# Reordering the two ends of a fused gradient kernel: power tables and dense layer moved into the FFT phase, row products moved into the first inverse

## The chip, the cores and the metric

The kernel runs on one core of a Trainium2 chip. The metric is the device time of one execution in microseconds (us). The kernel is one program of some 20,000 instructions on five engines: TensorE (PE; its weight loads are shown apart as PEld), VectorE (DVE), ScalarE (ACT), GpSimd (POOL) and SyncE (SP). Each engine has its own stream of instructions. The kernel's author writes one sequence of operations; a scheduler then decides, from that sequence and a plan of times of its own, in which order the instructions stand on each engine. So a change in the sequence can move instructions on engines that it does not mention.

## The reference

The forward function mixes two branches by a gate, and the reference returns its output together with the gradients for 14 inputs. L = 2048 positions, D = 448 channels, N = 256 states, F = 1792 hidden features.

```python
def _A_ref(u, A_re, A_im, B_re, B_im, C_re, C_im, log_dt, Dskip):
    dt = jnp.exp(log_dt)[:, None]
    ...
    P = jnp.exp(logdA[:, :, None] * l[None, None, :])      # powers of lambda
    K = jnp.einsum("dn,dnl,dn->dl", Cc, P, dB).real        # one kernel of L taps per channel
    ...                                                    # zero-padded FFTs of K and u
    y = irfft2(Uf * Kf)[..., :L]
    return y.transpose(0, 2, 1) + u * Dskip

def _B_ref(x, w1, b1, w2, b2):
    h = jnp.einsum("bsd,df->bsf", x, w1) + b1
    r = jnp.where(h > 0, h, 0)
    return jnp.einsum("bsf,fd->bsd", r * r, w2) + b2

g = _sigmoid((x * gate_w).sum(-1, keepdims=True))
out = g * _A_ref(x, ...) + (1 - g) * _B_ref(x, ...)

def reference(...):
    _out, _vjp = jax.vjp(_f, A_u, A_A_re, ..., gate_w)
    return (_out, *_vjp(grad_out))
```

## The kernel before

The kernel runs in phases:

1. *Front*: load u, the gate, DA = g x grad_output; an FFT in two layers of u and of DA, each layer going through DRAM (`fwd1` writes `gd`, `fwd2` reads it back); their product, and the inverse in two layers (`inv1` writes `hd`, `inv2`), give dk, the gradient of the kernel's taps. Beside it the raw parameters are turned into lambda and its powers (`powers`), which go to DRAM as records `rec_d`.
2. *Channel loop*: 14 blocks of 32 channels. For each, tables X and Y of powers are built by doubling (VectorE), the taps K are made from them (`kgen`, TensorE), and the gradients for the states are contracted with dk (`back_z`, `back_p`). Between these the dense branch runs forward and backward (`hidden`, `project`, and the weight gradients `grad_w2`, `grad_w1`).
3. *Tail*: FFT of K, two inverses (the output y, and the gradient of u), the parameter gradients, and some sums over rows.

The order of the front, cut to what the change touches (F17, K28, X16 and so on are buffers in on-chip memory that several tiles share in turn; a new tile of a name waits until the old one is no longer read):

```python
    for g in range(NG):                                   # u: four loads of 32 rows
        (nc.sync if g % 2 == 0 else nc.scalar).dma_start(flat(U[32 * g:32 * g + 32]), tl(u2, g))
    ...
    for t in range(LT):                                   # L362: the gate's row sums
        V.scalar_tensor_tensor(out=junk[:, 0, :], in0=U[:, t, 0:D], scalar=1.0, in1=gw_bc[:], ..., accum_out=s32[:, t:t + 1])
    S.activation(g_b[:], s_b[:], ACT.Sigmoid)             # L365
    for t in range(LT):
        last_da = V.tensor_scalar(out=DA[:, t, :], in0=G[:, t, :], scalar1=g32[:, t:t + 1], ...)
    ...
    K.act_only = True                                     # ScalarE alone empties the banks
    K.fwd1(lambda j: U[:, j, 0:D], gd[0], stage[0])
    K.act_only = False                                    # ScalarE and VectorE in turn (L171, L172, L181, L183)
    K.fwd1(lambda j: DA[:, j, :], gd[1], stage[1])
    transposed(U, None)
    ...
    for nm, src in (("Ar", A_A_re), ...):                 # raw parameters into X16
        nc.sync.dma_start_transpose(out=r, in_=src)
    ...                                                   # some 15 us of VectorE work on X16, Y16: L453 to L475
    for t in range(LT):
        S.activation(DB[:, t, :], G[:, t, :], ACT.Copy, scale=omg32[:, t:t + 1])
    transposed(DB, DBT_d)
    S1t = [K.t("X16", [P, 8192]), K.t("Y16", [P, 8192])]  # the buffers of fwd2's loads
```

The dense layer's first half, the powers and the loop over the four quarters of the spectrum:

```python
    def hidden(j):
        for l2 in range(2):
            for lc in (2 * l2, 2 * l2 + 1):
                ps = K.ps(NT[nti % 3], [P, 512])          # three accumulation banks in turn: N0, N1, N2
                ... T_.matmul(ps[:], lhsT=w1w[...], rhs=UT[...]) ...       # L501, L504
            for k in range(2):
                S.activation(RX[rxi % 3][...], pss[k][:], ACT.Relu, bias=b1_f[:, j:j + 1])   # L507
            G_.dma_start(... rT_d ..., RX[rxi % 3])
    psets = [(Fp[:, 0:4 * RS], ...), (RA[:, 0:4 * RS], ...)]   # powers' buffers: F17, and part of R32

    def powers(gr):
        rb, cb, qb = psets[gr % 2]
        ...
        for k in range(NLEV):                             # 11 levels, ScalarE and VectorE in turn
            S.copy(dst..., x)                             # L551
            if k < NLEV - 1:
                S.activation(sq, x, ACT.Square)           # L554
                V.scalar_tensor_tensor(...)               # L555
                V.tensor_tensor(...)                      # L556
        nc.scalar.dma_start(... rec_d ..., R)

    def spectra(q):
        for w in range(2):
            s1 = s1r[n1 % 4]
            K.load_s1(gd[w], q, s1)                       # L205
            K.fwd2(s1, q, spw[:, 2 * (q % 2) + w])        # L215
            ...
    spectra(0)
    for q in range(4):
        if q < 3:
            spectra(q + 1)
        K.cmul(Pc, ...)                                   # L227 to L232
        K.inv1(Pc, q, hd[0])                              # L246
        powers(q)
    dk_tl = K.t("D16", [P, LT, D])
    DK = K.t("K28", [P, 32, D])
    for q in range(4):
        hs = s1r[n1 % 4]...
        K.load_hs(hd[0], q, hs)
        ... K.inv2(...); K.evac2(dk_tl[...], ps)          # L264
    for rep in range(2):                                  # L599: dk spread over the partitions
        for g in range(NG):
            (nc.sync if rep == 0 else G_).dma_start(DK..., dk_tl...)
    for j in range(4):
        hidden(j)
```

The channel loop, in outline (L626, L627, L632 are the three products of a doubling; L684 is `kgen`; L713 and L726 empty the turned tables; L743 scales dk; L754 and L757 are `back_z`, L776 and L785 `back_p`):

```python
    for c in range(NCH + 1):
        ... seeds_x(c); ax = build_x(c); tables_t(c, 0)
        ... back_p(c - 1, ..., back_z(c - 1, YTs[c - 1], (0, 1)), ...)
        for half in range(2):
            ay = build_y(c, half, ap or ax)
            if half == 1:
                k_out(c, kgen(c))
            YTs[c] += [(turn_yt if g == 3 or c in (0, NCH - 1) else load_yt)(g) for g in (2 * half, 2 * half + 1)]
        ...
    for j in range(4, FT):
        hidden(j)
```

The tail's rows and inverses:

```python
    for g in range(NG):
        nc.sync.dma_start(flat(Gt[32 * g:32 * g + 32]), tl(G2, g))
    GU = K.t("Y16", [P, LT, D])
    V.tensor_tensor(out=GU[:], in0=Gt[:], in1=Uv, op=ALU.mult)          # L1148
    for t in range(LT):
        T_.matmul(ps[0:1, 0:D], lhsT=omg_b[:, t:t + 1], rhs=Gt[:, t, :], ...)   # L1152
    for t in range(LT):
        T_.matmul(ps[0:1, 0:D], lhsT=g_b[:, t:t + 1], rhs=GU[:, t, :], ...)     # L1157
    GK = K.t("Y16", [P, LT, D])
    V.tensor_tensor(out=GK[:], in0=Gt[:], in1=dskb, op=ALU.mult)        # L1161
    ...
    for q in range(4):                                                  # first inverse: the output
        for x in range(2):
            for hp in range(2):
                K.inv2(hs, q, x, hp, ps, [(ident[:], A[:, t, :]), (negI[:], br)])   # L262, L264
                V.scalar_tensor_tensor(out=jk, in0=ps, in1=Gt[:, t, :], ..., accum_out=dg[:, t:t + 1])  # L1185
                V.scalar_tensor_tensor(out=A[:, t, :], in0=ps, scalar=g32[:, t:t + 1], in1=br, ...)
        if q < 2:
            product(1, q + 2, sx[q + 2])
        ...
    for q in range(4):                                                  # second inverse, with GK: gradient of u
        ...
```

Of the kernel before, what the change touches and what calls it, by code (L numbers as in the profile page):

```python
# [129 lines left out]
class Ker:  # L130
# [56 lines left out]
    def fwd1(self, rhs, gd, stage):  # L187
        nc = self.nc
        for hh in range(2):
            for q in range(4):  # L190
                st = stage[self.stage_i % len(stage)]
                self.stage_i += 1
                for j2 in range(2):
                    ps = self.pair()
                    for jj in range(2):
                        nc.tensor.matmul(ps[jj][:, 0:D], lhsT=self.F1[:, hh * 128:(hh + 1) * 128], rhs=rhs(q * 4 + j2 * 2 + jj), start=True, stop=True)
                    self.evac2(st[:, 2 * j2:2 * j2 + 2, :], ps)
                j0base = 32 * hh + q * 4
                for g2 in range(2):
                    dst = bass.AP(tensor=gd, offset=(j0base + 16 * g2) * 64 * D, ap=[[D, 64], [64 * D, 4], [1, D]])  # L200
                    (self.q2 if g2 == 0 else nc.sync).dma_start(dst, st[g2 * 64:(g2 + 1) * 64])

    def load_s1(self, gd, q, s1):
        src = bass.AP(tensor=gd, offset=8 * q * D, ap=[[32 * D, 128], [1, 8 * D]])
        self.nc.sync.dma_start(s1.rearrange("p a d -> p (a d)"), src)  # L205
# [64 lines left out]
def kernel(ctx, tc, A_u, A_A_re, A_A_im, A_B_re, A_B_im, A_C_re, A_C_im, A_log_dt, A_Dskip,  # L270
# [54 lines left out]
    for g in range(NG):  # L325
        (nc.sync if g % 2 == 0 else nc.scalar).dma_start(flat(U[32 * g:32 * g + 32]), tl(u2, g))
# [9 lines left out]
    load_const("M2", nc.scalar)  # L336
# [61 lines left out]
    K.act_only = True  # L398
    K.fwd1(lambda j: U[:, j, 0:D], gd[0], stage[0])
    K.act_only = False  # L400
    K.fwd1(lambda j: DA[:, j, :], gd[1], stage[1])
    transposed(U, None)
# [7 lines left out]
    o = 0  # L410
# [3 lines left out]
    prm = [K.t("X16", [P, 8192]), K.t("Y16", [P, 8192])]  # L414
    raw = {}
    o = 0

    def carve(n, dt=bf16, k=0):
        nonlocal o
        w = n * (2 if dt == fp32 else 1)  # L420
        if k:
            r = prm[k][:, 0:w]
        else:
            r = prm[0][:, o:o + w]
            o += w
        return r.bitcast(fp32) if dt == fp32 else r
    for nm, src in (("Ar", A_A_re), ("Ai", A_A_im), ("Br", A_B_re), ("Bi", A_B_im), ("Cr", A_C_re), ("Ci", A_C_im)):
        r = carve(2 * D).rearrange("p (h d) -> p h d", h=2)
        nc.sync.dma_start_transpose(out=r, in_=src)
        raw[nm] = r  # L430
# [45 lines left out]

    for t in range(LT):
        S.activation(DB[:, t, :], G[:, t, :], ACT.Copy, scale=omg32[:, t:t + 1])
# [13 lines left out]
    def hidden(j):  # L492
        nonlocal nti, rxi
        for l2 in range(2):
            pss = []
            for lc in (2 * l2, 2 * l2 + 1):
                ps = K.ps(NT[nti % 3], [P, 512])
# [68 lines left out]
    def spectra(q):  # L566
        nonlocal n1
        for w in range(2):
            s1 = s1r[n1 % 4]
            n1 += 1  # L570
            K.load_s1(gd[w], q, s1)
            sp = spw[:, 2 * (q % 2) + w]
            K.fwd2(s1, q, sp)
            dst = bass.AP(tensor=sp_d[w], offset=q * 4 * 2 * D, ap=[[16 * 2 * D, P], [1, 8 * D]])
            nc.scalar.dma_start(dst, sp.rearrange("p a r d -> p (a r d)"))
    spectra(0)
    for q in range(4):
# [5 lines left out]
        powers(q)  # L583
    dk_tl = K.t("D16", [P, LT, D])
    DK = K.t("K28", [P, 32, D])
    for q in range(4):
        hs = s1r[n1 % 4].rearrange("p (g x) d -> p g x d", g=4)
        n1 += 1
# [13 lines left out]
    for j in range(4):  # L602
        hidden(j)
# [113 lines left out]
    def turn_yt(g):  # L717
# [4 lines left out]
        for h in range(2):  # L722
            pt = K.ps("X", [P, CW, P], bf16)
# [80 lines left out]
    for c in range(NCH + 1):  # L804
# [13 lines left out]
        for half in range(2):  # L818
            if c < NCH:
# [4 lines left out]
                YTs[c] += [(turn_yt if g == 3 or c in (0, NCH - 1) else load_yt)(g) for g in (2 * half, 2 * half + 1)]  # L824
# [5 lines left out]
    for j in range(4, FT):  # L830
        hidden(j)
# [109 lines left out]
    for g in range(NG):  # L941
        G_.dma_start(U[32 * g:32 * g + 32, :, 0:D], tl(u2, g).rearrange("p (t d) -> p t d", d=D))
# [54 lines left out]
    for j in range(FT):  # L997
        grad_w2(j)
    for j in range(JS):
# [147 lines left out]
    GU = K.t("Y16", [P, LT, D])  # L1147
    V.tensor_tensor(out=GU[:], in0=Gt[:], in1=Uv, op=ALU.mult)  # L1148
    row = K.t("st", [1, 3, D], bufs=2)
    ps = K.ps("N0", [P, 512])  # L1150
    for t in range(LT):
        T_.matmul(ps[0:1, 0:D], lhsT=omg_b[:, t:t + 1], rhs=Gt[:, t, :], start=(t == 0), stop=(t == LT - 1))  # L1152
    S.copy(row[:, 0], ps[0:1, 0:D])
    nc.sync.dma_start(out_13.rearrange("(o d) -> o d", o=1), row[:, 0])
    ps = K.ps("N1", [P, 512])
    for t in range(LT):
        T_.matmul(ps[0:1, 0:D], lhsT=g_b[:, t:t + 1], rhs=GU[:, t, :], start=(t == 0), stop=(t == LT - 1))  # L1157
    S.copy(row[:, 1], ps[0:1, 0:D])
    nc.sync.dma_start(out_9.rearrange("(o d) -> o d", o=1), row[:, 1])
    GK = K.t("Y16", [P, LT, D])  # L1160
    V.tensor_tensor(out=GK[:], in0=Gt[:], in1=dskb, op=ALU.mult)  # L1161
# [9 lines left out]
    brq = [load_br(0, 0), load_br(0, 1)]  # L1171
    for q in range(4):
# [16 lines left out]
        if q < 2:  # L1189
            product(1, q + 2, sx[q + 2])  # L1190
        sl = lambda a: a[:].rearrange("p (h q x) -> p q h x", h=2, q=4)[:, q]
# [69 lines left out]
```

## Time and profile before

| quantity | value |
|---|---|
| three timed executions | 1044.84, 1050.16 and 1068.91 us, median 1050.16 |
| the profiled execution | 1046.11 us, its span 1044.3 us |
| mean granted TensorE clock | 0.825 of full speed |
| bytes moved by DMA | 189.24 MB, mean 181 GB/s |
| fewest bytes a packet | 89473 of 151682 packets are under 512 B |

A line of the profile that speaks of an operation names its line in the kernel (L626), the engine, the operation and the tiles as "written <- read". Tiles are named by the first letters of their buffer (F for F17, K for K28, psN for a bank N0 to N3, psX for the bank X). Waits are put down to the operation whose end released the waiting one. A slice of the page's overview is a fortieth of the span, 26.1 us, and its digit gives the busy share in tenths.

### The profile page before, as it was taken

To read this page: it belongs to the slowest core of one execution; us is meant where nothing else is said; L and a number is where in the kernel's file an instruction comes from. 1 tells how busy PE (TensorE), PEld (TensorE's weight loads), DVE (VectorE), ACT (ScalarE), POOL (GpSimd) and SP (SyncE) were. 2 spreads that over 40 slices of the span, in tenths; PEclk is the share of its full clock that TensorE was granted. 3 is DMA by queue.
4 is the path that set the end of the run, shared out by engine and by line. 5 is a ranking of instruction groups with operands and counts; after the bars stand their busy time and mean duration, and the time that the engine had idled before them with its cause. 6 is when DMAs were issued, how large, how long until landed. Compare 5 with 4: busy or idle time off the path is not lost.

```text
span 1044.3 us, 20210 instructions
## 1 busy us (share of the span) xinstructions
PE 765.4 (73%) x8201; PEld 367.3 (35%) x8201; DVE 828.0 (79%) x1150; ACT 692.2 (66%) x1053; POOL 212.3 (20%) x358
## 2 busy tenths in 40 slices
PE   3655642649896898889889886078888976777886
PEld 1222210124343454444344334044545533323322
DVE  3588986584999989979799889189999678997470
ACT  0795558648878897677466646188687756765445
POOL 1330000101121221513423332002112421211120
PEclk9766555569898999789899987569899997889978
DMA  8979557972469557355956869742653679669788
GB/s 210 236 214 382 202 190 214 229 216 87 120 162 155 154 144 159 117 132 170 171 131 171 129 172 134 124 93 78 144 128 117 191 259 351 191 223 280 198 252 219
DMA packets 151682, 189.24 MB, mean 181 GB/s; under 512 B 89473, under 2 KB 124341, under 8 KB 150565
## 3 DMA queue, kind: packets, MB, share of 16 engines
q1 hardware_dynamic: 107956, 78.36, 33.9%
q0 software_dynamic: 24656, 78.65, 26.0%
q10 hardware_dynamic: 18976, 30.94, 8.5%
q8 instruction: 64, 1.05, 0.5%
q14 instruction: 30, 0.24, 0.1%
HBM read 94.45 MB, written 69.54 MB: 157 GB/s over the span
## 4 chain that ended last, share of the span: by engine, by line
DVE 33%; DMA 20%; PE 20%; ACT 14%; issue 10%; POOL 2%; SPq 0%; ACTq 0%; DVEq 0%; POOLq 0%
DVE F L627 5%; DMA R<-Y 4%; DVE P L776 3%; DVE Y L626 2%; DVE X L626 2%; ACT R L757 2%; PE psN L846 2%; DMA K<-D 2%; DVE Y L632 2%; DVE X L632 2%; DMA s_d<-st 2%; PE psX L684 2%; DMA gd<-F 2%; DMA R<-br_d 2%; DVE R L1071 1%
## 5 line engine op out<-in xcount | busy, mean ns | idle before, releaser
L757 ACT CAST R<-psF 128x1024 bf16<-128x1024 f32 x112 | 115.0, 1027 | 34.3 <-PE psF L754 32.4
L776 DVE TENSOR_TENSOR P<-R 128x2048 bf16<-128x2048 bf16 x84 | 98.0, 1219 | 37.1 <-ACT R L757 37.1
L846 PE MATMUL psN<-D,S 128*128 128x448 bf16 x448 | 107.0, 376 | 13.2 <-ACT D L847 10.1
L713 ACT COPY R<-psX 128x1024 bf16<-128x1024 bf16 x56 | 57.1, 1019 | 40.7 <-PE psX L712 40.4
L626 DVE TENSOR_TENSOR Y<-Y,F 128x256 bf16<-128x256 bf16 (+2 forms) x84 | 72.7, 866 | 2.3
L632 DVE TENSOR_TENSOR Y<-Y,F 128x256 bf16<-128x256 bf16 (+2 forms) x84 | 72.6, 864 | 2.2
L626 DVE TENSOR_TENSOR X<-X,F 128x512 bf16<-128x512 bf16 (+3 forms) x56 | 64.9, 1160 | 9.6 <-ACT F L653 7.8
L627 DVE TENSOR_TENSOR F<-Y,F 128x256 bf16<-128x256 bf16 (+2 forms) x84 | 72.0, 857 | 0.5
L969 PE MATMUL psN<-D,S 128*128 128x448 bf16 x224 | 55.9, 380 | 15.0 <-ACT S L964 11.2
L632 DVE TENSOR_TENSOR X<-X,F 128x512 bf16<-128x512 bf16 (+3 forms) x56 | 64.9, 1159 | 1.7
L627 DVE TENSOR_TENSOR F<-X,F 128x512 bf16<-128x512 bf16 (+3 forms) x56 | 64.5, 1151 | 0.1
L969 PEld LDWEIGHTS <-S 128*128 128x128 bf16 x448 | 41.4, 104 | 63.9 <-issue 20.9
L501 PE MATMUL psN<-S,U 128*128 128x512 bf16 x168 | 52.8, 428 | 14.7 <-ACT S L507 5.7
L846 PEld LDWEIGHTS <-S 128*128 128x128 bf16 x448 | 40.5, 102 | 62.7 <-issue 30.5
L754 PE MATMUL psF<-R,K 64*32 64x256 bf16 x672 | 38.0, 353 | 33.1 <-DMA R<-Y 26.9
L921 PE MATMUL psN<-S,U 128*128 128x512 bf16 x168 | 50.0, 421 | 6.2 <-ACT S L926 6.2
L969 PE MATMUL psX<-U,S 128*128 128x449 bf16 x192 | 48.5, 395 | 4.3 <-ACT S L964 4.3
L754 PEld LDWEIGHTS <-K 64*32 64x32 bf16 x896 | 25.8, 152 | 73.6 <-issue 42.3
L712 PE MATMUL psX<-ident,X 128*128 128x128 bf16 x448 | 39.8, 235 | 14.2 <-DVE X L632 8.0
L785 PE MATMUL psS<-P,cb_sel 128*32 128x256 bf16 x336 | 44.5, 285 | 1.5 <-DVE P L776 1.2
L785 PE MATMUL psN<-P,cb_sel 128*32 128x256 bf16 x336 | 45.3, 286 | 0.0
L726 ACT COPY M<-psX 128x1024 bf16<-128x1024 bf16 x28 | 28.7, 1026 | 19.1 <-PE psX L725 19.1
(332 smaller groups left out, 1898.1 us busy)
## 6 DMA issues: line engine op xcount, KB each, us to landing
hd<-st ACTq DMA_DIRECT2D x20, 448.0 KB, 5.4
sp<-K ACTq DMA_DIRECT2D x8, 896.0 KB, 8.3
S<-rT_d POOLq DMA_DIRECT2D x8, 896.0 KB, 6.9
dhT_d<-S POOLq DMA_DIRECT2D x28, 256.0 KB, 4.0
S<-rT_d POOLq DMA_DIRECT2D x14, 512.0 KB, 4.4
S<-dhT_d POOLq DMA_DIRECT2D x14, 512.0 KB, 6.1
R<-sp SPq DMA_DIRECT2D x8, 896.0 KB, 5.5
R<-hd SPq DMA_DIRECT2D x16, 448.0 KB, 6.8
```

Source lines behind the costliest of these rows:

```text
L501: T_.matmul(ps[:], lhsT=w1w[:, dt, j * P:j * P + P], rhs=UT[:, dt, 512 * lc:512 * lc + 512], start=(dt == 0), stop=False, skip_group_check ...
L626: V.tensor_tensor(out=hi, in0=lo, in1=bcast_dims(pr, [0, (None, n // 2), 1]), op=ALU.mult)
L627: V.tensor_tensor(out=Vv.rearrange("p (x a q) -> p x a q", x=rows, q=2), in0=lo, in1=bcast_dims(pi, [0, (None, n // 2), 1]), op=ALU.mult)
L632: return V.tensor_tensor(out=T4[:, :, :, n:2 * n], in0=T4[:, :, :, n:2 * n], in1=V4, op=ALU.add)
L713: S.copy(XT[:, gg].rearrange("p t i n -> p (t i n)"), pt[:].rearrange("p a n -> p (a n)"))
L754: T_.matmul(psz[32 * ii:32 * ii + 32, t, 256 * s:256 * s + 256], lhsT=(DK[64 * t:64 * t + 64, :, d] if s == 0 else DKB[64 * t:64 * t + 64, ...
L757: S.copy(zb[:, :, :, i2, :], psz[:].rearrange("p t (s n) -> p t s n", s=2))
L776: lastp = V.tensor_tensor(out=pr.rearrange("p t s i n -> p t s (i n)"), in0=zv, in1=(xb if r == 0 else rev_dim(xb, 1)), op=ALU.mult)
L785: T_.matmul(sps[s][32 * gr:32 * gr + 32, r, :], lhsT=sel[:, k, off:off + 32], rhs=Q[r][:, t, s, i2, :], start=(g < 2 and cc == 0 and i2 == ...
L846: T_.matmul(ps[:, 0:D], lhsT=hblk[j][:, P * tt:P * tt + P], rhs=ws[:, j, :], start=(w == 1 and j == 0), stop=(j == FT - 1))
L921: T_.matmul(ps[:], lhsT=w2Tw[:, jp, dt, j % 2], rhs=dblk[:, dt], start=(dt == 0), stop=False, skip_group_check=True)
L969: T_.matmul(ps[:, 0:width], lhsT=hh[:, t, :], rhs=(DB2[:, t, :] if w == 0 else U[:, t, 0:D + 1]), start=(t == 0), stop=(t == LT - 1))
```

## The change

It has four aims: to begin the gate sooner (u comes in two halves, and five of the eight stages of its first FFT layer are emptied by ScalarE alone, the others by both engines), to give VectorE its parameter work before the second `fwd1`, to bring the powers and the first four parts of the dense layer into the FFT phase, on the two banks X and S that this phase leaves free, and to take work on grad_output off the start of the tail's first inverse.

```diff
-    for g in range(NG):
-        (nc.sync if g % 2 == 0 else nc.scalar).dma_start(flat(U[32 * g:32 * g + 32]), tl(u2, g))
+    for h in range(2):
+        for g in range(NG):
+            src = bass.AP(tensor=u2.tensor, offset=u2.offset + (16 * g + 8 * h) * D, ap=[[64 * D, 32], [1, 8 * D]])
+            (nc.sync if g % 2 == 0 else nc.scalar).dma_start(flat(U[32 * g:32 * g + 32, 8 * h:8 * h + 8]), src)
 ...
-    load_const("M2", nc.scalar)
+    for nm, src in (("Ar", A_A_re), ("Ai", A_A_im), ...):      # moved here from below
+        nc.sync.dma_start_transpose(out=r, in_=src)
+    load_const("M2", nc.sync)
 ...
-    K.act_only = True
-    K.fwd1(lambda j: U[:, j, 0:D], gd[0], stage[0])
-    K.act_only = False
-    K.fwd1(lambda j: DA[:, j, :], gd[1], stage[1])
-    transposed(U, None)
+    K.fwd1(lambda j: U[:, j, 0:D], gd[0], stage[0], 5)         # act_only for the first 5 stages
 ...                                                            # the parameter work
+    K.fwd1(lambda j: DA[:, j, :], gd[1], stage[1])
+    transposed(U, None)
     for t in range(LT):
         S.activation(DB[:, t, :], G[:, t, :], ACT.Copy, scale=omg32[:, t:t + 1])
 ...
-    def hidden(j):
+    def hidden(j, banks):
-                ps = K.ps(NT[nti % 3], [P, 512])
+                ps = K.ps(banks[nti % len(banks)], [P, 512])
 ...
-            K.load_s1(gd[w], q, s1)
+            K.load_s1(gd[w], q, s1, G_ if w == 0 and q < 2 else None)
 ...
+    powers(0)
     spectra(0)
+    powers(1)
     for q in range(4):
         ...
         K.inv1(Pc, q, hd[0])
-        powers(q)
+        if q < 2:
+            powers(q + 2)
+    for j in range(4):
+        hidden(j, NT[4:6])                                     # banks X and S
     ...
-        hs = s1r[n1 % 4].rearrange("p (g x) d -> p g x d", g=4)
-        n1 += 1
+        hs = spw[:, q].rearrange("p a r d -> p (a r) d").rearrange("p (g x) d -> p g x d", g=4)
 ...
-    for j in range(4):
-        hidden(j)
 ...
-                YTs[c] += [(turn_yt if g == 3 or c in (0, NCH - 1) else load_yt)(g) for g in (2 * half, 2 * half + 1)]
+                for g in (2 * half, 2 * half + 1):
+                    YTs[c].append(turn_yt(g, ("S", "N3")) if c == 0 else turn_yt(g) if g == 3 or c == NCH - 1 else load_yt(g))
 ...                                                            # gradient phase: the second load of u
-    for g in range(NG):
-        G_.dma_start(U[32 * g:32 * g + 32, :, 0:D], tl(u2, g).rearrange("p (t d) -> p t d", d=D))
     for j in range(FT):
         grad_w2(j)
+        if j == 8:
+            for g in range(NG):
+                G_.dma_start(U[32 * g:32 * g + 32, :, 0:D], tl(u2, g).rearrange("p (t d) -> p t d", d=D))
 ...                                                            # tail
-    GU = ...; the 16 + 16 row matmuls and their outputs; GK = ...     # before the first inverse
     for q in range(4):
         ...
         if q < 2:
             product(1, q + 2, sx[q + 2])
+        if q == 1:
+            GU = ...; the 16 + 16 row matmuls and their outputs
+        if q == 3:
+            GK = ...
```

## The prediction

> **What bounds the kernel now.** I read first the page's busy shares and its 40 slices, to find which engine is nearly full and where it is not.
>
> ```profile
> PE 765.4 (73%) x8201; PEld 367.3 (35%) x8201; DVE 828.0 (79%) x1150; ACT 692.2 (66%) x1053; POOL 212.3 (20%) x358
> DVE  3588986584999989979799889189999678997470
> PEclk9766555569898999789899987569899997889978
> ```
>
> No engine is full, VectorE (DVE) is nearest. One digit stands for 26.1 us. From slice 10 to slice 32 VectorE stands at 7 to 9 except for one slice (number 25, 653 to 679 us). The change touches little there. What it does touch are slices 0 to 9 (0 to 261 us) and the last three. So I took the busy time of these stretches (columns: PE, PEld, DVE, ACT, POOL with counts, clock, DMA share, GB/s):
>
> ```profile
> 0.00:16.00 16.00, 0.18 (x1) 0.13 (x2) 0.32 (x3) 1.28 (x1) 3.06 (x11) 1.00 0.85 178
> 16.00:40.00 24.00, 15.29 (x77) 6.73 (x76) 16.80 (x57) 9.48 (x20) 4.72 (x5) 0.79 0.99 223
> 40.00:60.00 20.00, 13.93 (x69) 6.09 (x67) 14.03 (x25) 18.50 (x32) 8.42 (x14) 0.78 0.98 282
> 105.00:165.00 60.00, 34.76 (x120) 9.59 (x118) 54.37 (x108) 37.10 (x65) 0.00 (x0) 0.50 0.51 193
> 165.00:202.00 37.00, 12.54 (x77) 2.94 (x78) 17.32 (x47) 25.48 (x54) 1.75 (x4) 0.50 0.88 240
> 228.00:246.00 18.00, 16.63 (x118) 6.52 (x119) 3.18 (x3) 17.05 (x26) 3.50 (x7) 0.89 0.51 180
> ```
>
> VectorE works 169.6 us in the first 246 us: the six rows above hold 106.0 us of it, the three rows between them (60 to 82, 82 to 105 and 202 to 228) 17.9, 20.5 and 25.2. It idles 76 us, which is the whole room of the front part. Then the waits of that stretch say what ended the idle time (engine, line, what it waited for, total, times, longest):
>
> ```profile
> DVE X L640 <- PE psX L684: 16.9, 1, 16.9
> DVE st L362 <- DMA U<-in_A_u_dram: 14.9, 1, 14.9
> DVE R L172 <- PE psN L196: 9.8, 2, 9.4
> ACT g_b L365 <- DVE s_b L364: 17.3, 1, 17.3
> ACT F L653 <- DMA rec_d<-F: 7.2, 1, 7.2
> SPq L205 <- DVE X L469: 14.9, 1, 14.9
> ```
>
> Last the chain of waits, in order of time, which shows why the first channel block's kernel rows (L684) come at 245.9:
>
> ```profile
> 184.79 12.39 DMA rec_d<-F
> 204.78 21.62 DMA K<-D
> 229.10 6.83 DMA rT_d<-S
> 245.89 2.23 PE psX L684 x127
> ```
>
> The reader is to see a chain, not a full engine: a store of power records holds the buffer F until 197.2; the evacuations of dk stand behind that wait in ScalarE's order; then the spread of dk (K from D) takes 21.6 us; then ScalarE's scaling of it (L743), the dense layer's relus and the turned tables come before L684. VectorE has finished table Y at 231.3 and starts the next table X at 248.1.
>
> [...] ScalarE idles 17.3 us behind the sigmoid (L365) although the banks it is to empty next were filled by 18.2 us. So the order of instructions on an engine is itself the thing that this change edits. [...] here the granted clock is 0.50 from 105 to 202 us, and the second FFT layer's matmul of 448 columns takes 580 ns there, while a dense-layer matmul of 512 columns takes 379 ns at its median. [...] with a DMA share of 0.98 from 16 to 60 us I give the two loads moved to GpSimd nothing. [...] the trace has 1219 ns (L776), and 3.89 us for the two products of the tail, so moving those saves a place in line, not work.
>
> **The change, part by part.** I looked also at the order of the changed program's instructions on each engine. Nothing is added in arithmetic; everything is a matter of place.
>
> (1) u in two halves. The load takes 13.9 us to 15.6. If half the bytes land in half that time, the 16 row sums of the gate (0.67 us each) start near 9 us. Eight are done when the second half lands; the other eight with four transposition copies between them (0.69 each) end at about 15.6 + 8 x 0.67 + 4 x 0.69 = 23.7, against 29.2. Worth 5 us, if the load of grad_output, issued right behind, does not mix in.
>
> (2) Parameters before the second first-layer FFT. VectorE idled 9.4 us until the first of these banks (34.1 to 43.5). Now about 15 us of parameter work stands there, and the raw parameters are fetched before the constant M2. It also releases the buffers X and Y: the loads of the second layer waited 14.9 us for L469. But the DMA share is 0.98 in this time, and the 3.7 MB of that layer's own store move later. I take 8 us.
>
> (3) Powers ahead. From 105 to 202 VectorE works 54.4 + 17.3 = 71.7 of 97 us. Groups 2 and 3 of the powers ended that stretch alone, in turns with ScalarE at 0.76 us of waiting per level, and the store of group 2 held buffer F, which cost the start of table X 7.8 us. In the changed order groups 0 and 1 stand before and among the first evacuations, 2 and 3 among the complex products; the tables follow at once. Of the 25 us idle I expect 15 back; the rest is the inverse's own chain.
>
> (4) Dense layer on X and S, dk and kernel rows. L684 now stands on TensorE before the first use of dk, and L743 on ScalarE behind the rows' output. So the 16.9 us wait should all but go, but dk is still needed for the first P product (L776, at 262.3, which is 60.7 us after table X began at 201.7). Count in the new order from the start of table X: two X tables at 14 us, Y at 14.4, L684 at 2.2 make 45. For dk: of the eight pairs of dense-layer banks (four calls, two each) seven stand on TensorE just ahead of dk's matmuls or among them. Such a pair, with only two banks, is filled and emptied in turn: 8 matmuls x 0.38 = 3.0 us plus 0.65 for a relu, 3.7 us; the seven are 26 us from about 3 us before table X, with the inverse's matmuls some 32 us. Add 21.6 for the spread and 4 for scaling, matmul and evacuation: 55. So P comes at about 55 instead of 60.7: worth 6 us, not 17. Against this I set 6 us for the two banks in place of three and for orders that fit the chip less well than the planner thought.
>
> Front: 5 + 8 + 15 + 6 - 6 = 28 us.
>
> (5) The later load of u in the gradient phase. In the new order three of its four pieces still stand in the old place; one moves behind two other loads. The stall of slice 25 is a transposing transfer of Y (40.7 us for three, in the busiest time of the DMA engines) and I expect it to stay: 0.
>
> (6) Tail. grad_output lands at 963.2. The product with u (3.89 us) then came before the first L1185, and 32 row matmuls (2 x 3.2 us), of which the second 16 need that product, stood on TensorE before the second tile; VectorE waited 11.2 us at L1185. In the new order the first tiles come at 963 and the rows after the last inverse products. But these rows and then the product with the skip row (3.89) now stand before the third quarter: what is won at 967 to 979 (about 12) is partly given back near 1000 (6.4 + 3.9 at most, less where VectorE waited there anyway, 3.9). After 1016 the end belongs to loads: 10.5 and 6.1 us of R from br_d stand in the chain. Worth 5 us.
>
> Sum: 28 + 0 + 5 = 33. I start from 1047, between the two lower times (1044.8 and 1050.2), since the third (1068.9) stands apart: 1047 - 33 = 1014.
>
> **The rivals.** *The dk chain takes over.* If the dense layer on two banks is slower, say at the halved clock (634 ns is the longest of its matmuls, so 5.7 us a pair), dk arrives some 14 us later and P stands there; parts (3) and (4) give 7 instead of 21, and the time is 1028. For it: the clock was 0.50 there. Against it: the dense layer itself keeps TensorE busy; it had 0.89 from 228 to 246. *DMA bounds the front.* Loads, stores and transposes are the same bytes, and from 16 to 60 us they fill the engines; then (1) and (2) give nothing and the time is 1027. Against it: from 105 to 165 the share is only 0.51, so a late start is not lost twice. *The front moves more than counted.* VectorE's work before table X is 141 us; with no idle after 9 us it would begin at 150, not at 201.7. If two thirds of that idle went, 35 us instead of 28 and more at L684: 1000. *The middle eats it.* The blocks of channels meet other transfers at other times; the stall of slice 25 may grow or shrink by 10 us.
>
> **Range and chances.** The rivals span 1000 to 1028, and the middle adds 10 on either side. I take 990 to 1038 for 8 in 10. Faster by over 2% means under 1029: 0.74. Within 2%: 0.22, if two rivals meet. Slower: 0.04, only if the static order makes a new stall of 50 us.
>
> **What would show it.** Right: the first row sum near 9 us and the sigmoid by 24 (1); no idle of 9 us before the first-layer banks (2); table X's first L626 before 185 (3); the wait of L640 on psX under 5 us, and the first P product 52 to 60 us after that L626 (4); the first L1185 with no 11 us wait after it, last VectorE work 5 us nearer the end (6). Wrong: a wait of L776 or of ScalarE on K from D over 10 us (dk chain); first row sum still near 15; a stall in slices 22 to 26 of another length than 60 us.

## The result, and the profile after

The changed kernel took 1014.99 us (median of 5, 1012.12 to 1055.01) beside 1054.88 us for the kernel before on the same chip (median of 5, 1044.84 to 1068.91). The ratio is 0.966, with a 95% interval of 0.959 to 0.973; ratios here and below are of the fast runs alone, those within 1.5% of their kernel's fastest, while medians are of all runs. Measured a second time, it took 1023.99 us beside 1058.21. So the gain is 34 to 40 us, and the two sets of the changed kernel are themselves 9 us apart. The profile below is of the second set of runs; its span is 1022.3 us. The profiled execution of the first set is the one of 1055.01 us, in which the changed kernel took as long as the kernel before; it comes back below as "changed, first set".

From the page of the changed kernel, the busy shares, and the digits of VectorE and of the granted clock in slices of 25.6 us:

```profile
PE 776.2 (76%) x8201; PEld 366.6 (36%) x8201; DVE 827.0 (81%) x1155; ACT 689.1 (67%) x1048; POOL 213.2 (21%) x360
...
DVE  4788887676998899989789899688999479995750
...
PEclk9857555797898899899799997579999988879997
```

VectorE does the same work as before, 827.0 us against 828.0, in a span 22.0 us shorter than the profiled one of the kernel before. The hole of slice 25, counted from 0, is a 6 in this execution where the kernel before had a 1. The stretches of the front, with the columns of the prediction's table:

```profile
40.00:60.00 20.00, 15.01 (x63) 5.65 (x62) 17.61 (x34) 18.50 (x31) 6.77 (x11) 0.76 0.75 221
...
105.00:165.00 60.00, 31.35 (x109) 8.93 (x109) 49.17 (x104) 39.28 (x74) 0.00 (x0) 0.50 0.63 242
165.00:202.00 37.00, 27.27 (x124) 7.77 (x122) 25.81 (x38) 22.99 (x42) 4.33 (x8) 0.73 0.84 257
...
228.00:246.00 18.00, 8.14 (x65) 3.64 (x63) 11.14 (x8) 8.26 (x10) 1.66 (x2) 0.62 0.60 186
```

VectorE gains 3.6 us at 40 to 60, 8.5 at 165 to 202 and 8.0 at 228 to 246, and has 5.2 less to do at 105 to 165. In the first 246 us it now works 183.0 us, 13.4 more than before. TensorE works 27.3 us between 165 and 202, where it worked 12.5: the dense layer has moved in. The waits of the first 262 us:

```profile
DVE P L802 <- ACT R L783: 9.9, 2, 7.8
...
DVE st L390 <- DMA U<-in_A_u_dram: 9.6, 1, 9.6
...
PE psF L780 <- DMA K<-D: 8.2, 1, 8.2
...
ACT S L769 <- DMA K<-D: 7.0, 1, 7.0
...
DVE X L666 <- PE psX L710: 4.7, 1, 4.7
```

The wait for the first kernel rows (L684 is L710 here) fell from 16.9 to 4.7 us. New are the waits on K from D and, behind them, that of the first product P (L776 is L802). What happens between dk's arrival and P is in TensorE's timeline (start, us, what):

```profile
236.59 0.69 PE L780 MATMUL psF<-R,K 64*32 64x256 bf16 x8 [8.20 <-DMA K<-D]
237.73 0.43 PE L780 MATMUL psF<-R,S 64*32 64x256 bf16 x4 [0.45 <-ACT S L769]
...
240.71 1.46 PE L515 MATMUL psN<-S,U 128*128 128x512 bf16 x3
242.10 0.61 PE L518 MATMUL psN<-S,U 64*128 64x512 bf16 x1
...
245.43 0.41 PE L780 MATMUL psF<-R,K 64*32 64x256 bf16 x8
```

dk has landed at 236.6, but dense-layer matmuls (L515, L518) and turns of table X (L738, not shown) still stand between the first and the second group of contractions (L780); P starts at 247.1.

The traces can be reduced to five instants and a stretch. "Last output" is the last matmul of the dense layer's outputs (L846 of the kernel before), "first gradient" the moment at which TensorE comes to the matmuls of the first weight gradient (L969; the first of them starts up to 4.0 us later), both of the *dense stream*; P is the product (L776) of the *channel loop*. "Stretch" is the time from the start of table X of the eleventh block to that of the twelfth; in it the tenth block is contracted and the hole of slice 25 lies. Without a stall it takes 38.6 us (e6, e7). All in us, of the profiled execution; the two columns with a minus sign are differences.

| kernel | first P | last P | last output | first gradient | end | end − last P | last P − last output | stretch |
|---|---|---|---|---|---|---|---|---|
| before | 262.3 | 840.5 | 635.2 | 690.6 | 1044.3 | 204 | 205 | 63.4 |
| changed (e1) | 247.1 | 815.7 | 615.2 | 662.1 | 1022.3 | 207 | 201 | 50.5 |
| changed, first set (1055.01 us) | 247.8 | 842.4 | 628.7 | 691.7 | 1053.2 | 211 | 214 | 70.5 |
| e2 tail alone | 263.8 | 849.7 | 631.9 | 699.7 | 1057.2 | 208 | 218 | 71.6 |
| e3 without the dense move | 251.3 | 833.3 | 668.2 | 703.1 | 1055.9 | 223 | 165 | 45.3 |
| e4 without powers ahead | 256.4 | 814.9 | 634.1 | 678.2 | 1031.0 | 216 | 181 | 43.4 |
| e5 without early parameters | 256.7 | 816.4 | 619.2 | 666.9 | 1026.2 | 210 | 197 | 52.2 |
| e6 changed, block 10 by TensorE | 251.2 | 817.2 | 624.4 | 662.0 | 1024.9 | 208 | 193 | 38.6 |
| e7 before, block 10 by TensorE | 264.8 | 826.1 | 634.8 | 671.7 | 1033.7 | 208 | 191 | 38.6 |
| e8 changed, u load early | 245.5 | 847.4 | 621.5 | 691.8 | 1055.7 | 208 | 226 | 75.8 |
| e9 before, u load late | 261.3 | 829.2 | 631.2 | 679.5 | 1035.5 | 206 | 198 | 55.7 |
| e10 four gradients less | 248.1 | 809.6 | 620.8 | 657.2 | 1020.3 | 211 | 189 | 38.6 |
| e11 half the products | 250.9 | 769.4 | 687.6 | 723.6 | 1046.9 | 278 | 82 | 37.0 |
| e12 other gradients first | 247.1 | 812.2 | 624.6 | 642.1 | 1022.0 | 210 | 188 | 38.7 |

Before to changed (e1): the first P comes 15.2 us sooner. The stretch with the stall takes 50.5 instead of 63.4 us. The last P comes 24.8 sooner, so the rest of the loop gives back 3.4; the end comes 22.0 sooner, so the tail gives back 2.8. But the stall differs between executions of one kernel: in the other one of the changed kernel the stretch takes 70.5 us, and the last P comes 1.9 us later than before although the first came 14.5 sooner.

### The profile page after: what moved, and what is told of

The parts are those of the page before. It is cut to its first block, busy times and chain, and to the rows that moved or that the text cites. A ratio compares the mean times of both kernels' runs of the same rounds, so it can differ in the third digit from the quotient of the medians.

```text
span 1053.2 us, 20218 instructions
## 1 busy us (share of the span) xinstructions
PE 774.6 (74%) x8201; PEld 366.5 (35%) x8201; DVE 827.7 (79%) x1155; ACT 689.2 (65%) x1048; POOL 213.1 (20%) x360
## 5 line engine op out<-in xcount | busy, mean ns | idle before, releaser
L759 ACT CAST R<-psF 128x1024 bf16<-128x1024 f32 x112 | 114.7, 1024 | 19.6 <-PE psF L756 17.8
L756 PE MATMUL psF<-R,K 64*32 64x256 bf16 x672 | 38.6, 354 | 46.0 <-DMA R<-Y 31.8
L924 PE MATMUL psN<-S,U 128*128 128x512 bf16 x168 | 50.3, 423 | 13.8 <-ACT S L929 13.8
L501 PE MATMUL psN<-S,U 128*128 128x512 bf16 x120 | 38.3, 430 | 7.8 <-ACT U L507 3.5
L756 PE MATMUL psF<-R,S 64*32 64x256 bf16 x672 | 34.7, 299 | 9.0 <-issue 8.7
```

Of the source, the lines that this page charges most:

```text
L756: T_.matmul(psz[32 * ii:32 * ii + 32, t, 256 * s:256 * s + 256], lhsT=(DK[64 * t:64 * t + 64, :, d] if s == 0 else DKB[64 * t:64 * t + 64, ...
L759: S.copy(zb[:, :, :, i2, :], psz[:].rearrange("p t (s n) -> p t s n", s=2))
L924: T_.matmul(ps[:], lhsT=w2Tw[:, jp, dt, j % 2], rhs=dblk[:, dt], start=(dt == 0), stop=False, skip_group_check=True)
```

## Experiments

The runs e1 to e4 set the prediction (theory A, the gain comes from the two ends) against theory B, that it comes from the middle. Theory C, formed on their traces, said that the dense stream sets the end: in the kernel before and in e1 to e4 the end stands 353 to 360 us behind the first weight gradient. Its rival was that the channel loop sets the end. Each part of the change was taken out or put in alone. The runs e1 to e4, e5 to e8 and e9 to e12 are three sets; the changed kernel was measured only in the first of them and with the result, so that what e5 to e12 differ from it by is not clear of noise below some 9 us.

**e1: the changed kernel again.** No edit.

> The changed kernel once more, unchanged, for a second trace. Theory A (the gain comes from the two ends, as predicted, and the middle runs as before): 1010 to 1018 us; table X begins near 183 us and the first P product stands near 248; the distance between the tenth and eleventh block's first VectorE instruction, 63.5 us before, stays 58 to 66; the tail from the last block on is 15 to 20 us shorter than the 263.8 us of before. Theory B (the gain comes from the middle, the transposing transfers of Y meeting fewer other transfers): the same total, but that distance is under 50 us and the tail is shorter by less than 8.

Measured: 1023.99 us (1023.44 to 1031.2, 4 runs) beside 1058.21 (1034.41 to 1060.64, 7 runs); e2 to e4 share these runs of the kernel before, of which one took 1034.41 and the other six 1054.28 or more. The gain stands. Theory A is right in the front (table X at 182.1, first P at 247.1) and fails behind it: the stretch is 50.5 us and not 58 to 66, and the tail from the last block's table X on is 266.6 us where it was 263.4, and not 15 to 20 shorter. Theory B is nearer.

**e2: the tail alone,** in the kernel before.

```diff
-    GU = ...; the 16 + 16 row matmuls; GK = ...      # before the first inverse
+        if q == 1: GU = ...; the row matmuls
+        if q == 3: GK = ...
```

> The kernel before with the tail's part of the change alone. Theory A: the tail is shorter by 5 us as predicted, up to 20 if the two ends carry all of the gain, so 0.980 to 0.995 of before. Theory B: under 3 us, 0.997 to 1.0.

Measured: 1059.08 us (1056.93 to 1060.13), 0.9 above the kernel before. TensorE's timeline of the changed kernel after the first two output tiles (L1185 of the kernel before; VectorE takes them from 937.8 to 939.6) shows why the tail gives nothing:

```profile
936.27 3.41 PE L997 MATMUL psX<-U,S 128*128 128x449 bf16 x16 [0.23 <-ACT S L992]
...
944.17 3.21 PE L997 MATMUL psX<-U,S 128*128 128x449 bf16 x16 [0.32 <-ACT S L992]
...
950.25 1.50 PE L997 MATMUL psX<-U,S 128*128 128x449 bf16 x7 [0.34 <-ACT S L992]
...
951.87 0.37 PE L267 MATMUL psN<-R,cb_Etw 64*32 64x448 bf16 x4
```

The rows are gone, but matmuls of three weight gradients of the dense layer (L997) stand before the third tile (L267), and VectorE waits 12.7 us there, where it waited 11.2 before the second. In this trace none of the third tile's matmuls runs among them: the first (L265, not shown) starts at 951.59, and the last group of L997 at 950.25.

**e3: without the dense move.** The four parts of the dense layer stand behind dk again, on three banks, and the first block's turned tables are on one bank again.

```diff
-    for j in range(4): hidden(j, NT[4:6])            # before dk's inverse
+    for j in range(4): hidden(j, NT[0:3])            # behind the spread of dk
```

> The changed kernel with the first four dense-layer parts put back behind dk, on three banks, and the first turned tables on bank X alone; powers ahead, early parameters and tail stay. My step (4) net of the two banks was 0 to 6 us: 1014 to 1021 us, table X near 183 as in the changed kernel, and the wait of the second X table on the kernel rows back above 10 us. If the dense layer on two banks delays dk (rival), the first P product comes earlier here than in the changed kernel and the time is at or under 1014.

Measured: 1057.22 us (1055.24 to 1061.23): 33 us of the changed kernel's gain are gone. One line of its trace, the output matmuls (durations in ns, then the first and last start):

```profile
L874 PE MATMUL psN<-D,S x448: 352/353/581, 334.2 to 668.2; 128*128 128x448 bf16 x150
```

They begin 23.8 us later than in the changed kernel (310.4): the four parts are back in the loop's time. They also last 29.2 us longer (334.0 against 304.8), and the reason is an order: on TensorE the taps of ten channel blocks stand before the last output matmul, in the kernel before and in the changed one of nine. So the 33 us, where 0 to 6 were expected, are the dense work and a block that changed places, and not the dense work alone. A longer stall is no part of them: the stretch takes 45.3 us here. The first P comes 4.2 us later than with the move.

**e4: without the powers ahead.**

```diff
-    powers(0); spectra(0); powers(1); ...            # and powers(q + 2) for q < 2
+    spectra(0); ... powers(q)                        # behind each quarter's inverse
```

> The changed kernel with the powers of each group back behind the inverse product of their quarter; the rest stays. My step (3) was 15 us: 1026 to 1032 us, with table X starting 12 to 19 us later than in the changed kernel. If the powers only changed places with the inverse's own chain, under 5 us.

Measured: 1032.59 us (1028.13 to 1042.88), 8.6 more. The first table X comes at 202.5 instead of 182.1, the first P 9.3 later, the last P at the same time, helped by a stretch that is 7.1 us shorter; the last output matmul comes 18.9 later, and as in e3 the taps of ten blocks stand before it. The end is 9 us further behind the last P than in e1, so in this trace the loss comes through the dense stream.

**e5: without the early parameters,** without u in halves, and with the loads of the first two quarters on the old issuing engine.

```diff
-    u in two halves; parameters before the second fwd1
+    u in one; parameters behind it
-    K.load_s1(gd[w], q, s1, G_ if w == 0 and q < 2 else None)
+    K.load_s1(gd[w], q, s1)
```

> The changed kernel with parts (1) and (2) undone: u in one piece, the raw parameters and the second first-layer FFT where they stood, all loads of the second layer issued by SyncE; powers ahead, dense layer early and tail stay. My steps (1) and (2) were 5 and 8 us: 1030 to 1040 against the changed kernel's 1024 of the last runs. A rival, that the front is bound by its bytes and the gate's start is hidden, gives 1024 to 1028. A third theory, formed on the runs so far (the dense stream, from the first relu to the last weight-gradient matmul, sets the end, and the channel loop only runs beside it), expects the time to follow the end of the dense layer's first half: 1024 plus what that end (300.1 us in the second trace of the changed kernel) moves.

Measured: 1021.51 us (1014.93 to 1028.41), 2.5 less than with them, which is not clear of noise; a loss of 6 to 16 us, as expected, is not there. The first P comes 9.6 us later, but the last P only 0.7: the loop absorbs it on the way (it is 8.8 us behind at the start of the third block, 4.1 at the eleventh).

**e6 and e7: no transposing transfers in the tenth block,** in the changed kernel and in the kernel before. Its tables are turned by TensorE, as in the first and last block.

```diff
-    ... turn_yt(g) if g == 3 or c in (0, NCH - 1) else load_yt(g)
+    ... turn_yt(g) if g == 3 or c in (0, NCH - 1, 9) else load_yt(g)
```

> The changed kernel with the tables Y of the tenth block turned by TensorE and emptied by ScalarE in place of the three transposing transfers that meet the loads of the gradient phase; 24 transposes and 6 evacuations of 1.02 us more, no arithmetic changed. If the stall of that place is this collision: no wait on R from Y above 5 us there, the distance of the tenth to the eleventh block from 50.5 to about 40, 8 to 15 us faster (1009 to 1016), and the single runs of this kernel within 8 us of one another. If the stall only follows from the gradient phase's own loads (matmuls waiting for grad_output): 0 to 3 us, and the wait moves to the operands of the weight gradients.

> The kernel before with the same replacement in the tenth block alone. If half of the change's gain was a shorter collision, then it closes here too: 1030 to 1042 us (before 1058 in the last runs), and the changed kernel with the replacement is only 1.5 to 2.5% under it. If the collision is a matter of chance on both sides, the gap between the two stays 3 to 3.5%.

Measured: 1025.13 us (1022.87 to 1028.02) and 1035.49 (1019.33 to 1045.26, 13 runs), beside 1057.55 for the kernel before (1036.53 to 1078.74, 32 runs). The kernel before gains 22 us, the changed one nothing: there the stretch falls from 50.5 to 38.6 us, but the one before it (tenth block to eleventh) grows from 43.5 to 54.5, which it does not in e7 (48.2, was 48.5); why was not tried. With the stall out of both the medians are 10 us apart instead of 34, and the traces 8.8. Even these 10 are not clear: the four runs of e6 lie inside the range of the thirteen of e7, and beside the kernel before the ratios are 0.983 (0.976 to 0.990) and 0.984 (0.977 to 0.992). So in the medians most of the 34 us are the stall.

**e8: the changed kernel with the load of u early, e9: the kernel before with it late.** That is part 5 taken out alone and put in alone.

```diff
     for j in range(FT):
         grad_w2(j)
-        if j == 8: the four loads of u
+    # e8: the four loads of u before this loop; e9: the other way round in the kernel before
```

> The changed kernel with part (5) undone: the second load of u stands again ahead of the weight gradients. In the order of instructions only one of its four pieces moves, ahead of two loads. My step (5) was 0 us: 1022 to 1027. If that piece is what lets the transposing transfers through, 8 us or more are lost, and the distance of the tenth to the eleventh block is near 60 us again.

> The kernel before with part 5 alone: the second load of u stands in the source after the ninth weight gradient; in the order of GpSimd's instructions this moves one 0.45 MB piece of u behind the first load of hidden features. Theory C (the stall of the tenth block is a collision of its three transposing transfers with the loads of the gradient phase, and the start of the weight gradients sets the end): the transfers take under 35 us together instead of 40.7, and the time falls by 8 to 20 us from the kernel before, to 1037 to 1049. Rival, the prediction's own term (three of four pieces stay put, the stall stays): within 4 us of the kernel before, near 1057. A further rival: the piece only matters at the moment at which the changed kernel's tenth block meets it, so that here the stall may even grow.

Measured: e8 1038.23 us (1026.56 to 1057.67, 21 runs), 14 more than the changed kernel's second set and 23 more than its first; e9 1036.83 (1025.29 to 1064.94, 4 runs) beside 1055.22 (1046.88 to 1066.62, 22 runs), 18 less, a ratio of 0.978 (0.966 to 0.990). In the order of GpSimd's instructions the fourth load of u (448 KB) stands behind two loads of hidden features (512 KB each) and two stores of 112 KB, or ahead of them. The three transposing transfers of the tenth block (R from Y) show the stall; each fence is one kernel's, the first line with the time that each issue took in ns, the second with the time from issue to landing. The kernel before:

```profile
L733 SPq DMA_TRANSPOSE R<-Y x3: 4024/5312/31198, 632.8 to 642.4; - x3
...
DMA to landing us min/median/max: 7.9/22.8/37.7
```

The changed kernel:

```profile
L759 SPq DMA_TRANSPOSE R<-Y x3: 3659/6070/17900, 616.2 to 626.1; - x3
...
DMA to landing us min/median/max: 10.3/16.8/23.2
```

The kernel before with the load late (e9):

```profile
L767 SPq DMA_TRANSPOSE R<-Y x3: 3497/5769/23944, 629.4 to 638.9; - x3
...
DMA to landing us min/median/max: 8.3/9.9/11.4
```

The changed kernel with it early (e8; its profiled execution is the slowest of its 21):

```profile
L760 SPq DMA_TRANSPOSE R<-Y x3: 2833/23244/25968, 621.6 to 647.9; - x3
...
DMA to landing us min/median/max: 12.2/20.7/29.2
```

The changed kernel in the execution of 1055.01 us, the load late:

```profile
L735 SPq DMA_TRANSPOSE R<-Y x3: 3907/4199/26520, 626.0 to 634.3; - x3
...
DMA to landing us min/median/max: 8.3/26.8/45.3
```

From the start of the first issue to the end of the third it takes 40.7 us before, 27.8 in the changed kernel, 33.4 in e9, 52.2 in e8 and 34.8 in the last one. The three issues follow one another, and contractions and products wait: TensorE 23.2, 18.4, 17.9, 39.1 and 31.8 us on R. The plain loads of grad_output in the same place take longer as well. Their time from issue to landing (median, the last number), in the kernel before and then in e7, without the three transfers:

```profile
D<-in_grad_out_dram POOLq DMA_DIRECT2D x4, 448.0 KB, 26.5
```

```profile
D<-in_grad_out_dram POOLq DMA_DIRECT2D x4, 448.0 KB, 6.2
```

So the stall that the prediction left in place goes with the three transfers: without them the stretch takes 38.6 us in both e6 and e7, and the loads of grad_output land in 6.2 us in e7, where they took 26.5 with them. Part 5 alone moves the medians by 14 to 18 us (by e9's interval 11 to 36). But the place of that load does not decide alone: in the execution of 1055.01 us it is late, and the stretch takes 70.5 us, more than the 63.4 of the kernel before. One trace of each kernel cannot show how the place acts.

**e10: four weight gradients less,** on top of e6. The loads, transpositions, squares, matmuls and copies of the last four of the 14 second-layer gradients are left out; their outputs hold another gradient's rows.

```diff
     for j in range(FT):
+        if j >= FT - 4: store the rows of an earlier gradient; continue
         grad_w2(j)
```

> The changed kernel with the tables of the tenth block turned by TensorE (as in the run without the collision, 1025), and without the work of the last four of the 28 weight gradients: their loads, transpositions, squares, matmuls and copies are left out, and their outputs hold another gradient's rows. Theory C: the weight gradients' stream sets the end; 28 parts take some 302 us, 10.8 us each, so four less give 20 to 43 us: 982 to 1005. Rival (the channel loop on VectorE sets the end, the dense stream runs beside it): under 8 us, 1017 to 1025.

Measured: 1013.15 us (1010.02 to 1022.42), 12 less than e6; its trace is of the slowest of the four. Both guesses miss. If the dense stream alone set the end, four parts of 10.8 us would have shown.

**e11: half the products P,** on top of e6. The second product of each pair is not computed, the first is used in its place.

```diff
             for r in range(2):
+                if r == 1: Q.append(Q[0]); continue
                 V.tensor_tensor(out=pr, in0=zv, in1=..., op=ALU.mult)
```

> The changed kernel with the tables of the tenth block turned by TensorE (1025), and with half of the products P of the state gradients left out: the second product of each pair is replaced by the first, so 56 of VectorE's products of 1.22 us are not made, 68 us of its work in 14 blocks, about 49 us of it before the weight gradients begin. Theory C: VectorE runs beside the dense stream, so 0 to 15 us: 1010 to 1025. Rival (channel loop on VectorE sets the end): 45 to 68 us, 957 to 980.

Measured: 1048.45 us (1039.03 to 1061.38, 20 runs): 23 *more* than e6, with 68 us less for VectorE to do. The products and the output matmuls of e6, then of e11 (two lines of each trace):

```profile
L802 DVE TENSOR_TENSOR P<-R x84: 1217/1219/1230, 251.2 to 816.1; 128x2048 bf16<-128x2048 bf16 x84
```

```profile
L873 PE MATMUL psN<-D,S x448: 349/353/581, 311.2 to 624.4; 128*128 128x448 bf16 x150
```

```profile
L807 DVE TENSOR_TENSOR P<-R x42: 1218/1220/1230, 250.9 to 765.5; 128x2048 bf16<-128x2048 bf16 x42
```

```profile
L878 PE MATMUL psN<-D,S x448: 349/353/581, 318.8 to 687.6; 128*128 128x448 bf16 x150
```

The channel loop does end 48 us sooner (last P 769.4 against 817.2), but the last output matmul comes 63 us later. The order of instructions shows why: the taps of twelve blocks stand on TensorE before the last output matmul instead of nine. That the scheduler did this because its plan has a shorter loop is inferred. The weight gradients then begin at 723.6 and the end is theirs.

**e12: the first layer's gradients first,** on top of e6, with the load of u early: two weight gradients that do not need grad_output fill the 38 us between the last output matmul and the first gradient. Nothing is left out.

```diff
+    for j in range(JS): grad_w1(j, NT[0:3])          # JS = 2
     for j in range(FT): grad_w2(j)
-    for j in range(JS): grad_w1(j, NT[0:3])
```

> The changed kernel with the tables of the tenth block turned by TensorE (1025), with u loaded early again, and with the two weight gradients of the first layer, which need u and not grad_output, put ahead of the fourteen of the second layer, which must wait for grad_output in the buffer that the second layer's output held (some 40 us between the last output matmul and the first weight-gradient matmul). No work is left out. Theory C: this gap of the dense stream is worth up to two parts of 10.8 us: 5 to 22 us less than 1025, so 1003 to 1020, which would beat both kernels. Rival: the parts wait for u or the channel loop bounds, 1022 to 1030.

Measured: 1023.29 us (1019.24 to 1029.97). The first gradient starts 20 us sooner than in e6 (642.1), and the last P only 5 us sooner; the end follows the last P. It is 1.8 us below e6 and no faster than the changed kernel, as the rival had it. No version that does all the work beats the changed kernel by more than the runs differ.

**What the fourteen traces say together.** Theory C in its strong form falls with e10, e11 and e12. In eleven traces the end stands 204 to 211 us behind the last P, and in these the last P is at least 188 us behind the last output matmul. In the three where that distance is under 185 (e3, e4, e11), the end stands 216 to 278 behind the last P. In these three the taps of ten (e3, e4) or twelve blocks (e11) stand on TensorE before the last output matmul, in the other eleven those of nine. This is the picture of two streams, the channel loop and the dense stream, threaded through one order of instructions on TensorE, where the later one sets the end. In the kernel before and in the changed one it is, by this reading, the channel loop; no run has shortened the loop alone with TensorE's order kept. The threshold is read off these traces, not derived, and e4 lies close to it.

## Why the prediction came true, and where its steps failed

The total was right (33 us predicted, 34 to 40 measured), in good part by luck; the steps were not right, and their errors cancel. By e6 and e7 most of the gain came from a stall that the prediction had at 0, and the front, which it had at 28, brought the first P 15.2 us forward.

*Start of the sum.* 1047 was low: other runs of the kernel before have medians of 1055 to 1058. The third time was set aside as standing apart, but it lay inside the spread seen later (1036.53 to 1078.74).

*(1) u in halves: mechanism right.* VectorE's wait for u ends at 10.3 us (was 15.6) instead of near 9, and the last work on the row sums begins at 25.7 (was 29.2): 3.5 us instead of 5.

*(2) and (3): right at the table, little of it at the end.* The wait of 9.4 us at the first-layer banks is gone, and table X starts at 182.1 (was 201.7): 19.6 of the 22 us that 5 + 8 + 15, less the 6 set against them, would give. (The 0.76 us of waiting per level of the powers is read from four levels; at others VectorE waited 0.24 to 0.84 us or not at all.) At the end, e5 puts (1) and (2) at nothing (−2.5 us), the two loads moved to GpSimd among them (that these alone give nothing was the author's estimate, and no run shows it), and e4 puts (3) at 8.6, with a block that changed places in it. The step that failed is "Front: 28 us" as a gain of the end: it took a start of the loop for its finish.

*(4): the path to P mis-sized, the work misplaced.* The wait on L684's bank fell to 4.7, as predicted. P was to come 55 us after table X, and came 65.0 (60.6 before), so that +6 was −4. The dk chain was counted well: 32 + 21.6 puts its landing 50.6 us after table X's start less 3, and it came at 54.5. The last term, "4 for scaling, matmul and evacuation", took 10.5, because of the dense-layer matmuls, relus and turns of table X between the two groups of L780. The rival of the dk chain was half right: waits of 8.2 and 7.0 us on K from D, under the 10 set as the mark. Its clock of 0.50 did not stay: from 165 to 202 the granted clock was 0.73, with TensorE at work for 27.3 us (0.50 and 12.5 us before); that the work brings the clock was the author's estimate, and no run shows it alone. Missed altogether was that the move takes four of the fourteen parts out of the loop's time; e3 shows the output matmuls 23.8 us later without it, and in all 33 us, with the change of order in them.

*(5): failed.* "The stall of slice 25 ... I expect it to stay: 0." The step argued that three of four pieces stay put; moving the fourth alone makes 14 (e8) to 18 us (e9). From the profile of the kernel before to that of e1 the stretch is 13.0 us shorter, and another length of the stall was one of the signs of being wrong that the prediction named. "The middle eats it" stood there with 10 us either way, as chance; it is both, a part of the change in the medians and chance in the single execution, where the stretch took 50.5 us once and 70.5 once.

*(6): failed.* Instead of 5 us, e2 finds −0.9, and the distance from the last VectorE work to the end is 28.0 us, as before. The 11.2 us wait was put down to row matmuls, and they were in TensorE's timeline before that tile; but some 7.5 us of it (968.1 to 975.6) are the weight gradients of L969 ahead of the rows, which the change does not move.

So the sum that was measured in the profiles of the kernel before and e1 is front 15.2, stall 13.0, rest of the loop −3.4, tail −2.8: 22.0. In the medians it is 34, the kernel before having been profiled in an execution near the low end of its spread. The losses with a part taken out (33 in e3, 14 in e8, 8.6 in e4) add up to far more than 34, so they are not shares of the gain.

## What to carry to other kernels

Where two streams of work share an engine's static order, book a saving only on the stream that ends last, and ask what the scheduler does with the time freed: here 68 us less work made the kernel 23 us slower. A stall seen in one slice can be part of the change when a transfer near it changes places (here one load of 448 KB, worth 14 us in e8 and 18 in e9 in the medians); take it out of both kernels once to see how much of a difference is the stall, and read more than one execution: here two of one program differ by 20 us in this place. Read everything that stands in an engine's timeline before a late instruction, and not only what the change moves: here weight gradients stood on TensorE before the third tile of the tail, and VectorE waited 12.7 us.

## What was not expected of the hardware

Three transposing transfers issued next to plain loads of about 0.5 MB took 27.8 to 52.2 us from the first issue to the end of the third and up to 45.3 to land; eighteen of the same kind in the changed kernel between 300 and 560 us landed in 4.4 to 7.1 us, and its fourteen plain 512 KB loads of hidden features in 4.7 us at the median. In the tenth block the plain loads were slow too: those of grad_output, 448 KB each, took 16.7 to 40.7 us at the median (the kernel before, both executions of the changed one, e2, e5, e8), and 6.2 in e7, without the three transfers, where they were also issued further apart (over some 10 us, and within 1.5 in the kernel before). So the loss is not of the transposing transfers alone. Why the place of one load changes it was not tried.

The time of one program on one core spreads by several per cent: 1036.53 to 1078.74 us in 32 runs of the kernel before. The stall has a part in this, since the stretch took 50.5 and 70.5 us in two executions of the changed kernel, but it is not the whole: without the three transfers thirteen runs of e7 still spread from 1019.33 to 1045.26.
